# A list scheduler's ranks: program order before, latest begins from a backward walk after

## The chip, the cores and the metric

The kernel runs on one NeuronCore of a Trainium2 chip. The metric is the device time of one execution in microseconds; three runs of the kernel before give a median of 1071.82 us.

## The reference

Three stages follow each other; the first one's output is the second one's input, and so on.

```python
# attention: batch 4, heads 8, sequence 576, head size 64, float32
scores = q @ k.T / sqrt(64)
thresh = max(scores, axis=-1) - tau                 # tau = 0.02
scores = where(scores >= thresh, scores, -1e9)
attn   = exp(scores - max(scores)); attn /= sum(attn) + 1e-9
x      = (attn @ v)  -> (2304, 512)
# gated layer, weights 512 x 1536 (and 1536 x 512), float64 in memory
x = (sigmoid(x @ w_gate) * (x @ w_val)) @ w_out
# second layer, w1, w2: 512 x 1024, w3: 1024 x 1024, w_out2: 1024 x 512
out = ((x @ w1) * (x @ w2) @ w3) @ w_out2
```

## The kernel before

**Attention.** The 4 batches hold 4 pairs of heads each, so 16 pairs; a pair takes 9 steps (four blocks of 128 queries per head and one block of the tails), 144 steps in all, 36 a batch. A step g is: the scores on TensorE into one of two PSUM buffers (`s_mm`, L618), the row maximum less tau on DVE (`s_max`, L648), the threshold and the exponential on ACT (`s_exp`, L656 and L657), a split of the result into two f16 halves (`s_hi` on ACT at L668 or DVE at L666, `s_lo` mostly on POOL at L674), a transposing DMA (`s_tr`, L678), and five steps later the product with v (`pv`, L681). Each value of q, k and v is split in a high and a low part, which costs each pair some ACT, DVE and POOL work ahead of its steps (`q_act`, `q_dve`, `k_act`, `k_dve`, `v_max` to `v_split`). After 9 steps the pair is normalised (L699), transposed (L717) and written to `XA` (`x_act`, L732 and L734).

**Filler.** Between the parts of a step the program calls `filler` twice (L1217 and L1230), which emits other work for TensorE. First that is the product w3 @ w_out2 (`merge_gen`, L803), which takes 24 units of float64 weights, cast by DVE, ACT and POOL at L762 to L771 (`cast64`), and needs no attention. When all of it is emitted, its pool `mp` closes, and the pools of the gated layer open in its place (the planner's `over`). Then `l1_gen` (L903) emits the gated layer in passes: pass b works on batch b, and its first step, `xsplit` (L968), reads what `x_act` of batch b wrote. Pass 0 also casts the 36 units of the layer's float64 weights, at 2 POOL operations a unit (L771 and L781), and stores them as float32 for the passes after it. Pass 3 comes behind attention.

**The planner.** All instructions up to `cut` (L1231, the end of the attention loop with its fillers) are put in a new order by `Plan` (L22 to L304). `edges` finds the dependencies of the written program: `hard` ones (data and buffer reuse) and `soft` ones (order of allocation, and PSUM accesses of one engine). `time` has a cost for each operation. `order` (L207) walks forwards in time: of all engines it takes the one whose best instruction could start first; on an engine that is the instruction with the least wait until it is surely ready, and among those ready the one with the lowest `rank` (L229). The rank is the place in the written program, as `BY` is 0 (L50, L1125):

```python
self.rank = [n + by * (i.name in behind) for n, i in enumerate(self.x)]
...
n = min(avail[e], key=lambda n: (max(sure[n] - free[e] - 1, 0), self.rank[n]))
```

`pin` (L297) fixes the order found on each of the engines PE, DVE, ACT, POOL and on SP, which issues all DMAs. The order is worked out when the program is built; the chip runs each engine's list in that order, with semaphores for the dependencies.

Behind the cut come pass 3 of the gated layer, the splitting of w1 and w2, and the second layer. They are not planned by `Plan`.

Of the kernel before, what the change touches and what calls it, by code (L numbers as in the profile page):

```python
# [21 lines left out]
class Plan:  # L22
# [9 lines left out]
    CLK = 3413.0  # L32
    SLACK = {"DMACopy": 3000.0, "DmaTransposeAnt": 1500.0}
    HOLD = 200.0

    def __init__(self, insts, cut, over, late=(), by=0):
        self.later = [i for i in insts[cut:] if i.opcode in self.OPS]
        insts = insts[:cut]
        self.x = [i for i in insts if i.opcode in self.OPS and self.name(i.engine) in self.ENG]
        self.e = [self.ENG[self.name(i.engine)] for i in self.x]  # L40
        self.io = [
            ([o.bass_ap for o in i.ins if hasattr(o, "bass_ap")],
             [o.bass_ap for o in i.outs if hasattr(o, "bass_ap")])
            for i in self.x
        ]
        self.hard = [set() for _ in self.x]
        self.soft = [set() for _ in self.x]
        self.edges(over)
        behind = {insts[i].name for a, b in late for i in range(a, min(b, cut))}
        self.rank = [n + by * (i.name in behind) for n, i in enumerate(self.x)]  # L50
        self.cost = [self.time(n) for n in range(len(self.x))]

    @staticmethod
    def name(e):
# [119 lines left out]
    def time(self, n):  # L174
        x, e = self.x[n], self.e[n]
        ins, o = self.io[n][0], self.io[n][1][0]
        k = max(self.free(o), self.free(ins[0]) if ins else 0)
        sb = [self.place(a) != "PSUM" for a in ins] or [True]
        if e == "SP":
            if x.opcode == "DmaTransposeAnt":  # L180
                return 1440, 1152 * 18.8 / 16, 702, 1305, 1152
            c, r = self.packets(o, ins[0])
            one = max(r / (22.0 if r <= 2048 else 18.0) + 5, 48 if r >= 512 else 0) + (40 if c == 64 else 0)
            return 530, c * one / 16, 1055, 1285, c
        if e == "PE":
            f = all(str(a.dtype).endswith("float32") for a in ins)
            h = self.size(ins[0]) == 2
            iv = 29 if k <= 64 else 108 if f else 39 if h else k / 2.4 + 13
            return iv, 165 + iv, k / 2.4 * (2 if f else 1)
        if e == "ACT":  # L190
            ptr = len(ins) > 1
            return 167 + (30 if sb[0] else 0) + (85 if ptr and k > 1 else 60 if ptr else 0) + k / 1.2 + 95 * (
                len(self.io[n][1]) - 1
            ), 0, 0
        if e == "POOL":
            if len(ins) < 2:
                return 110 + 0.95 * k, 0, 0
            return (150 + 2.0 * k if self.size(o) == 2 else 160 + 2.2 * k), 0, 0
        if self.free(o) == 128 and k > 576:
            return 1280, 0, 0  # L200
        port = all(sb) and self.place(o) != "PSUM" and k > 1 and (
            x.opcode in ("TensorTensor", "TensorCopy") or self.size(ins[-1]) == 2
        )
        more = len(self.io[n][1]) > 1 or any(self.free(a) == 1 for a in ins)
        return 148 + (k / 0.96 + (60 if more else 0) if k > 1 else 0), port, 0

    def order(self):  # L207
# [16 lines left out]
        while left:  # L224
# [55 lines left out]
            for m in succ[n]:  # L280
                need[m] -= 1
                if not need[m]:
                    r = t = max((start[q] for q in self.soft[m]), default=0.0)
                    for q in self.hard[m]:
# [3 lines left out]
                        else:  # L288
                            u = done[q] + self.LAG[self.e[q]] + self.LEAD[self.e[m]]
                            r = max(r, u)  # L290
                            t = max(t, u + self.SLACK.get(self.x[q].opcode, self.HOLD))
                    ready[m], sure[m] = r, t
                    avail[self.e[m]].append(m)
        self.start, self.done = start, done
        return seq

    def pin(self, tc):  # L297
        for e, l in self.order().items():
            for m, n in zip(l, l[1:]):
                tc.add_manual_dep(  # L300
                    self.x[n], self.x[m].name,
                    mybir.DependencyInfo(mybir.DependencyClass.NoSync, mybir.DependencyReason.DATA),
                    reason="order",
                )  # L304
# [1198 lines left out]
```

## Time and profile before

| | us |
|---|---|
| median of three runs (lowest, highest) | 1071.82 (1071.23, 1078.38) |
| the profiled execution's own time | 1074.56 |
| its span, first to last instruction | 1072.8 |
| TensorE busy in the span | 1004.5 |
| VectorE (DVE), ScalarE (ACT), GpSimd (POOL) busy | 673.1, 663.7, 692.4 |

Busy times are sums over the span; what an engine is worth is read in each stretch by itself. [...]

### The profile page before, as it was taken

The numbers are of one execution on the slowest core, as the hardware profiler recorded it, in microseconds if no ns is written. First come the engines' busy times: TensorE is split into PE (matmuls) and PEld (weight loads), VectorE is DVE, ScalarE is ACT, GpSimd is POOL, SyncE is SP. The second block draws the span as 40 slices with busy tenths as digits, with TensorE's granted clock in tenths as the row PEclk, the third lists the DMA queues.
The fourth block names the chain that finished last, engine by engine and source line by source line (L and its number), as shares of the span: only waits on it lengthen the run. The fifth ranks groups of instructions, "written<-read, shape, count | busy, mean of one in ns | idle before, by whom it ended". The sixth has DMA issues, their size and how long they took to land. (4 is left out here: it accounts for less than half of the span.)

```text
span 1072.8 us, 20181 instructions
## 1 busy us (share of the span) xinstructions
PE 1004.5 (94%) x7088; PEld 891.5 (83%) x7088; DVE 673.1 (63%) x1226; ACT 663.7 (62%) x1325; POOL 692.4 (65%) x587
## 2 busy tenths in 40 slices
PE   4599976899998999999999989999999999999997
PEld 3488865687887888888888879999999989989995
DVE  8896587777866655557554447776776725743741
ACT  6687699978879878879887664445432322422221
POOL 5966288899997777667766756767664723552530
PEclk9999969999999999999999999999999999999999
DMA  8899699999999999989987675767378619835822
GB/s 218 237 238 226 146 234 220 254 224 268 252 251 228 219 211 223 209 191 210 232 171 164 130 178 186 255 223 236 129 248 276 204 60 321 258 98 173 310 78 59
DMA packets 301844, 221.28 MB, mean 206 GB/s; under 512 B 221872, under 2 KB 250544, under 8 KB 301744
## 3 DMA queue, kind: packets, MB, share of 16 engines
q1 hardware_dynamic: 301744, 220.00, 80.9%
q8 instruction: 56, 0.92, 0.4%
q14 instruction: 44, 0.36, 0.1%
HBM read 133.17 MB, written 30.93 MB: 153 GB/s over the span
## 5 line engine op out<-in xcount | busy, mean ns | idle before, releaser
L674 POOL TENSOR_TENSOR h<-e,h 128x576 f16<-128x576 f32 x120 | 155.1, 1295 | 75.7 <-ACT h L668 43.0
L648 DVE TENSOR_SCALAR_CACHE_REDUCE e<-ps_s,tauc 128x576 f32<-128x576 f32 x144 | 117.1, 814 | 72.2 <-PE ps_s L348 31.9
L656 ACT ACTIVATE ps_s<-ps_s,nt 128x576 f32<-128x576 f32 x144 | 102.4, 712 | 50.0 <-DVE e L648 48.4
L657 ACT ACTIVATE e<-ps_s,ebias 128x576 f32<-128x576 f32 x144 | 106.5, 740 | 2.9 <-POOL vl L781 0.4
L348 PEld LDWEIGHTS <-pt 128*128 128x128 f16 x2240 | 76.7, 100 | 32.6 <-issue 23.1
L348 PE MATMUL ps_h<-xl,gh 128*128 128x512 f32 (+1 forms) x240 | 93.1, 388 | 3.9 <-POOL xl L781 2.8
L348 PE MATMUL ps_h<-xl,vh 128*128 128x512 f32 (+1 forms) x240 | 92.5, 385 | 0.0
L348 PE MATMUL ps_y<-wm,abh 128*128 128x512 f32 x288 | 91.4, 390 | 0.3 <-DVE wm L781 0.3
L348 PE MATMUL ps_o<-gvl,oh 128*128 128x512 f32 (+1 forms) x240 | 90.7, 378 | 0.0
L348 PE MATMUL ps_h<-xh,gh 128*128 128x512 f32 (+1 forms) x240 | 89.1, 371 | 0.0
L348 PE MATMUL ps_h<-xh,gl 128*128 128x512 f32 (+1 forms) x240 | 88.9, 371 | 0.0
L348 PE MATMUL ps_h<-xh,vh 128*128 128x512 f32 (+1 forms) x240 | 88.8, 370 | 0.0
L348 PE MATMUL ps_h<-xh,vl 128*128 128x512 f32 (+1 forms) x240 | 88.8, 370 | 0.0
L348 PE MATMUL ps_o<-gvh,ol 128*128 128x512 f32 (+1 forms) x240 | 88.5, 369 | 0.0
L348 PE MATMUL ps_o<-gvh,oh 128*128 128x512 f32 (+1 forms) x240 | 88.3, 369 | 0.0
L668 ACT ACTIVATE h<-e 128x576 f16<-128x576 f32 x126 | 86.0, 684 | 2.9 <-DMA pt<-h 1.5
L781 POOL TENSOR_TENSOR gl<-w,gh 128x512 fp32r<-128x512 f32 x42 | 55.0, 1310 | 49.3 <-ACT gh L780 48.7
L781 POOL TENSOR_TENSOR gvl<-gr,gvh 128x512 fp32r<-128x512 f32 (+1 forms) x48 | 60.3, 1256 | 10.2 <-ACT gvh L780 9.6
L780 ACT ACTIVATE abh<-r 128x384 fp32r<-128x384 f32 x48 | 24.2, 521 | 68.9 <-DVE r L1368 68.6
L781 POOL TENSOR_TENSOR ol<-w,oh 128x512 fp32r<-128x512 f32 x42 | 55.8, 1336 | 16.7 <-ACT oh L780 16.7
L781 POOL TENSOR_TENSOR vl<-w,vh 128x512 fp32r<-128x512 f32 x43 | 58.1, 1352 | 8.7 <-ACT vh L780 8.4
L348 PEld LDWEIGHTS ps_y<-wm,abh 128*128 128x128 f32 x288 | 54.0, 188 | 11.4 <-DVE wm L781 0.6
(208 smaller groups left out, 3021.0 us busy)
## 6 DMA issues: line engine op xcount, KB each, us to landing
wc<-sc_c SPq DMA_DIRECT2D x168, 256.0 KB, 3.4
w<-sc_w SPq DMA_DIRECT2D x35, 768.0 KB, 5.2
sc_c<-wc SPq DMA_DIRECT2D x56, 256.0 KB, 2.7
XR<-in_moe_w_out_dram SPq DMA_DIRECT2D x20, 512.0 KB, 4.9
sc_w<-w SPq DMA_DIRECT2D x11, 768.0 KB, 5.9
XR<-in_moe_w_dram SPq DMA_DIRECT2D x16, 512.0 KB, 4.7
raw<-in_moe_w_dram SPq DMA_DIRECT2D x16, 512.0 KB, 4.6
XR<-in_moe_w_gate_dram SPq DMA_DIRECT2D x12, 512.0 KB, 5.5
```

Of the source, the lines that this page charges most:

```text
L348: nc.tensor.matmul(out_, lhsT, rhs, start=first, stop=last)
L648: nc.vector.tensor_scalar(e, x["ps"], tauc, None, op0=ALU.add, op1=ALU.min, accum_out=nt)
L656: nc.scalar.activation(x["ps"], x["ps"], AF.Prelu, scale=-1.0, bias=x["nt"], alpha=STEEP)
L657: nc.scalar.activation(x["e"], x["ps"], AF.Exp, bias=ebias, accum_out=prep[pr]["sum"][:, s:s + 1])
L668: nc.scalar.activation(x["h16"][:, 0:S], x["e"], AF.Copy)
L674: eng.tensor_tensor(hb[:, S:2 * S], st[g]["e"], hb[:, 0:S], op=ALU.subtract)
L780: nc.scalar.activation(hi, x, AF.Copy)
L781: (lo_eng or nc.gpsimd).tensor_tensor(lo, x, hi.bitcast(F32), op=ALU.subtract)
```

## The change

`Plan` gets a method `backward`, and `pin` runs `order` and `backward` in turn twice before the last `order`. `backward` schedules the same instructions in reversed time, from those with no successor, with the durations that the forward walk gave (`lat`) and the time for which each holds its engine (`held`). Of an engine's candidates it takes the one with the least wait, among equals the one that the forward walk finished last. The instructions are then sorted by how far before the end they must begin, and that place is their new `rank`. The rule by which `order` picks is unchanged, as are the instructions, the tiles, the buffers and everything behind the cut. Two more pieces come along: an argument `beads`, for which no caller passes anything, and a cost for matmuls with operands of 64 partitions.

```diff
+    ROUNDS = 2
-    def __init__(self, insts, cut, over, late=(), by=0):
+    def __init__(self, insts, cut, over, late=(), by=0, beads=()):
...
+        for row in beads:
+            row = [at[insts[i].name] for i in row]
+            for m, n in zip(row, row[1:]):
+                self.soft[n].add(m)
+                self.hard[n].discard(m)
...
+            if ins[0].ap[0][1] == 64 and k > 128:
+                side = ins[0].offset * self.size(ins[0]) // (ins[0].tensor.bytes() // 128) >= 64
+                return (4 if side else k / 2.4 + 11), 290, k / 2.4 * (0 if side else 1)
...
+    def backward(self):
+        N, E = len(self.x), ("PE", "DVE", "ACT", "POOL", "SP")
+        pred = [self.hard[n] | self.soft[n] for n in range(N)]
+        out = [0] * N
+        for n in range(N):
+            for q in pred[n]:
+                out[q] += 1
+        lat = [d - s for s, d in zip(self.start, self.done)]
+        held = [
+            c[0] if e in ("PE", "SP") else max(60, c[0] - self.OVER[e])
+            for c, e in zip(self.cost, self.e)
+        ]
+        ready, begin = [0.0] * N, [0.0] * N
+        avail = {e: [n for n in range(N) if not out[n] and self.e[n] == e] for e in E}
+        free = dict.fromkeys(E, 0.0)
+        for _ in range(N):
+            best = None
+            for e in E:
+                if not avail[e]:
+                    continue
+                n = min(avail[e], key=lambda n: (
+                    max(ready[n] + lat[n] - held[n] - free[e] - 1, 0), -self.done[n]
+                ))
+                s = max(free[e], ready[n] + lat[n] - held[n])
+                if best is None or s < best[0]:
+                    best = s, e, n
+            s, e, n = best
+            avail[e].remove(n)
+            begin[n] = free[e] = s + held[n]
+            for q in pred[n]:
+                out[q] -= 1
+                if q not in self.hard[n]:
+                    r = begin[n] - lat[q]
+                elif self.e[q] == self.e[n] != "SP":
+                    r = begin[n] - (lat[q] - 5 if e == "PE" else 0)
+                else:
+                    r = begin[n] + self.LAG[self.e[q]] + self.LEAD[e]
+                ready[q] = max(ready[q], r)
+                if not out[q]:
+                    avail[self.e[q]].append(q)
+        for i, n in enumerate(sorted(range(N), key=lambda n: -begin[n])):
+            self.rank[n] = i
+
     def pin(self, tc):
+        for _ in range(self.ROUNDS):
+            self.order()
+            self.backward()
         for e, l in self.order().items():
```

## Rows read from the trace of the kernel before

**Rows 1.** Page, its first part: busy us, share, instructions of each engine.

```profile
PE 1004.5 (94%) x7088; PEld 891.5 (83%) x7088; DVE 673.1 (63%) x1226; ACT 663.7 (62%) x1325; POOL 692.4 (65%) x587
```

**Rows 2.** Chain that ended last, in order of time: start us, us, what.

```profile
631.84 0.31 ACT XR L734
...
632.23 0.53 ACT xh L780
...
632.83 1.01 POOL xl L781
...
633.88 8.59 PE ps_h L348 x48
```

**Rows 3.** Windows view of the whole core, by stage.

```profile
core 0: us, PE busy (x) PEld busy (x) DVE busy (x) ACT busy (x) POOL busy (x), PEclk, DMA share, GB/s
0.00:50.00 50.00, 22.40 (x109) 19.06 (x110) 41.83 (x82) 32.66 (x62) 37.09 (x44) 1.00 0.82 224
50.00:100.00 50.00, 49.05 (x394) 41.91 (x393) 41.42 (x78) 40.97 (x80) 34.04 (x29) 1.00 1.10 231
100.00:125.00 25.00, 22.29 (x182) 19.04 (x181) 12.79 (x27) 16.89 (x35) 7.88 (x7) 0.93 0.80 189
125.00:178.00 53.00, 38.61 (x414) 34.45 (x413) 39.49 (x84) 46.86 (x96) 40.00 (x34) 0.81 0.96 210
178.00:225.00 47.00, 40.39 (x366) 33.71 (x363) 34.81 (x76) 43.45 (x92) 40.56 (x34) 0.96 1.09 239
225.00:325.00 100.00, 98.81 (x776) 82.47 (x775) 72.75 (x140) 79.68 (x158) 93.71 (x77) 1.00 1.06 254
325.00:350.00 25.00, 21.27 (x226) 17.70 (x224) 15.86 (x36) 23.60 (x50) 19.29 (x16) 0.93 1.07 222
350.00:475.00 125.00, 125.00 (x981) 103.12 (x977) 71.85 (x145) 101.17 (x201) 87.44 (x71) 1.00 1.02 212
...
500.00:625.00 125.00, 125.00 (x986) 102.63 (x985) 65.05 (x130) 97.80 (x194) 85.75 (x70) 1.00 0.85 179
...
632.50:1072.80 440.30, 431.50 (x2340) 412.26 (x2340) 258.99 (x394) 152.52 (x309) 224.65 (x195) 1.00 0.60 195
```

**Rows 4.** Windows view of line L648 alone (DVE); two instructions are one step.

```profile
50.00:75.00 25.00, 4.90 (x12) 1.00 1.07 238
...
125.00:150.00 25.00, 4.94 (x12) 0.82 0.80 185
150.00:175.00 25.00, 6.59 (x16) 0.78 1.12 234
```

**Rows 5.** Windows view of tile ps, the merge's PSUM banks.

```profile
50.00:75.00 25.00, 20.06 (x95) 14.96 (x93) 4.12 (x6) 4.63 (x8) 1.00 1.07 238
...
125.00:150.00 25.00, 4.57 (x18) 3.25 (x18) 0.00 (x0) 0.60 (x1) 0.82 0.80 185
```

**Rows 6.** Timeline of PE, 170 to 192 us: the first matmul of pass 0.

```profile
181.00 0.49 PE L348 MATMUL ps_h<-xl,gh 128*128 128x512 f32 x1
```

**Rows 7.** Waits of PE, 100 to 225 us: us in total, times, longest.

```profile
PE ps_s L348 <- ACT e L657: 8.0, 6, 1.8
PE ps_s L348 <- DVE qbd L515: 4.0, 2, 2.8
...
PE ps L348 <- DVE tl L847: 2.7, 1, 2.7
```

**Rows 8.** Waits, two of the longest by DMA or cast: DVE 100 to 125, PE 0 to 50.

```profile
DVE vm L568 <- DMA vnat<-in_v_dram: 4.0, 1, 4.0
...
PE ps L842 <- POOL f L771: 7.5, 1, 7.5
```

**Rows 9.** Lines L771 and L666: ns min/median/max, first and last start us.

```profile
L771 POOL TENSOR_TENSOR w<-w,t x36: 1249/1288/1498, 139.0 to 332.0; 128x512 int32<-128x512 int32 x36
...
L666 DVE CAST h<-e x18: 452/939/2944, 21.4 to 312.4; 128x576 f16<-128x576 f32 x18
```

**Rows 10.** Groups of POOL, 225 to 325 us.

```profile
L674 POOL TENSOR_TENSOR h<-e,h 128x576 f16<-128x576 f32 x21 | 27.5, 1316 | 3.7 <-ACT h L668 2.7 <-ACT t L767 0.5 <-DVE h L666 0.4
...
L781 POOL TENSOR_TENSOR vl<-w,vh 128x512 fp32r<-128x512 f32 x8 | 10.4, 1295 | 0.9 <-ACT vh L780 0.9
```

More of the change, by code (lines that the diff above doesn't have):

```diff
@@ L48, in __init__ @@
         self.edges(over)
+        at = {i.name: n for n, i in enumerate(self.x)}
+        for row in beads:
[3 more added lines that the diff above has]
+                self.hard[n].discard(m)
+        ends = set()
+        for row in beads:
+            ends |= {at[insts[row[1]].name], at[insts[row[-1]].name]}
         behind = {insts[i].name for a, b in late for i in range(a, min(b, cut))}
@@ L51, in __init__ @@
         self.cost = [self.time(n) for n in range(len(self.x))]
+        for n in ends:
+            self.cost[n] = self.cost[n][0] + 100, *self.cost[n][1:]
     @staticmethod
```

## The prediction

> **What bounds the kernel now.** I read the page's engine shares first: TensorE is busy for 94% of the span, no other engine for more than 65% [rows 1]. Whatever order the planner finds, TensorE's work stays, so what can be won is its idle time and the time that it runs at the lower clock. The chain comes next [rows 2]: it begins at 631.84 us with the last write of attention, goes through the split of that batch, and from 633.88 is TensorE alone. So the kernel's time is the end of attention plus a tail. The tail lies behind the cut; TensorE is busy for 431.5 of its 440.3 us [rows 3], and the planner does not touch it. I carry it over unchanged.
>
> The windows by stage [rows 3] then say where TensorE is idle in the planned part: 27.6 us in the first 50, 0.95 in 50 to 100, 2.7 in 100 to 125, 14.4 in 125 to 178, 6.6 in 178 to 225, 1.2 in 225 to 325, 3.7 in 325 to 350, and nothing in 350 to 475 or 500 to 625. Nearly all that an order can still mend lies before 350 us.
>
> Why is it idle there? The merge product is the only filler until batch 0 of attention is done. It takes 20.06 of 25 us early and its last 4.57 us fall in 125 to 150 [rows 5], while the next filler, pass 0, starts its first matmul at 181.00 [rows 6]. Between them TensorE has attention alone, and waits for ACT's exponential and for DVE [rows 7]; ACT is busy for 46.86 of 53 us [rows 3]. Attention makes 6 steps in 25 us while the merge runs, 8 when it has gone [rows 4]. So TensorE is full first and starved later. Pass 0, once it runs, loads another engine: POOL is busy for 93.71 of 100 us in 225 to 325 [rows 3].
>
> **The change, part by part.** No instruction is added or removed, so every term is a wait that goes, comes or moves. `beads` is never passed and costs nothing. The cost for operands of 64 partitions matches no matmul: those of pass 0, the merge and attention load all 128 rows (the 128*128 in [rows 6]). What is left is the ranks. The walk still never leaves an engine idle when something is surely ready, so a rank decides only between instructions that are ready together. I expect it to matter where four engines are all half full and queues are long, before 178 us, and little where TensorE is full anyway.
>
> *The stretch 50 to 178.* By program order, casts and merge matmuls emitted at step g go ahead of attention's step g+3. A latest begin puts ahead what has the longest way to the end: attention's chain of scores, maximum, exponential, split and transpose, and the casts of pass 0, and puts back what has slack. Every instruction that is moved takes its own DMAs along on SP. TensorE's idle time here is 0.95 + 2.7 + 14.4 = 18.05 us. As a check from the other side: the 24 steps of 50 to 150 at 6 in 25 us take 100 us; at 7 (half way to the 8 of [rows 4]) they would take 24/7 x 25 = 85.7, some 14 us less, of which the idle 18.05 has room. At the least nothing is won; at the most all 18; and if attention made 5.5 steps instead of 6, 24/5.5 x 25 - 100 = 9 us would be lost. I take half of the idle time, 9.0.
>
> *The stretch 178 to 350.* Idle are 6.6 + 1.2 + 3.7 = 11.5 us. Part of it is the end of pass 0 before batch 1 is done (325 to 350), which better balance would mend. POOL limits it: casts and splits of 36 units at about 1.29 us an operation run from 139 to 332 us [rows 9, 10], and no rank makes them shorter. I take a third, 4.0; bounds 0 and 11.5 for the gain; the loss is the second rival's.
>
> *The clock.* The granted clock is 0.93, 0.81, 0.96 and 0.93 in four of these stretches [rows 3]. [...] But there it waits for ACT and DVE, so faster matmuls only make the waits longer: I take 0 of 0 to 15.4, and keep it for the low end.
>
> *The first 50 us.* 27.6 us idle, the longest wait being 7.5 for a merge cast [rows 8]. Loads and the chain of the first pair set this; I take 0, between 7.5 won and 5 lost (one more wait like that for `qbd`, of which the longest was 2.8 [rows 7], on either of two pairs).
>
> *New stalls.* An order is as good as the planner's durations. Now DVE stands 4.0 us before `vm` for a load, with others queued behind it, and TensorE 2.7 us for `tl` [rows 7, 8]: both are waits in a fixed order that hardly any planner would choose. The new order loses these and gets others. I take them as equal: 0, within 6.7 either way.
>
> The sum: 9.0 + 4.0 = 13 us. The profiled execution took 1074.56 us, so 1061.6 for one like it; the median of the runs shown lies 2.7 below that execution, which makes 1058.8, say 1059.
>
> [...] The casts of L666 on DVE take 452 ns at best, 939 in the median and 2944 at worst [rows 9], with POOL at work beside the slow ones. [...]
>
> **Rivals.** *First: nothing that can be measured (within 1%, 10.7 us, is about what a measurement of this kernel can't tell from no change).* For it: ACT is 88% busy in 125 to 178, so batch 0 may be bound by ACT and not by order, and the walk already fills every gap that it sees. Against it: ACT has 9 us free in 50 to 100 and 8 in 100 to 125 [rows 3]. Then only a third of the terms comes, 4 us: 1068, from 1062 to 1078.
>
> *Second: slower, by POOL in pass 0.* Where: 225 to 325 us, POOL 93.71 of 100 busy, TensorE 98.81. Each unit of weights needs two POOL operations and each step of attention one more at L674 [rows 10]. If the ranks put attention's L674 ahead of a unit's split, TensorE stands at the next matmul for half an operation, 0.65 us, on average: 36 x 0.65 = 23 us, some of it at the lower clock. Less 9 us from the first term, 14 lost net: 1086. It decides from the point at which more than about 14 of the 36 units arrive late (14 x 0.65 = 9). For it: the 6% of slack. Against it: both walks know POOL's costs, and POOL is busy for only 41.9 of the 75 us from 50 to 125, so an order that starts pass 0's casts sooner eases it.
>
> *Third: the ranks come out as program order nearly does.* The program was emitted with attention and filler interleaved, and the reverse walk breaks ties by the forward one. Then 1071, within 4. Against it: 24 casts of the merge are emitted within few steps, long before they are due.
>
> **How the numbers follow.** The forecast 0.48, the first rival 0.24, the second 0.19, the third 0.09. The forecast's own range is 1042 to 1061. Toward the low end it would need the whole 29.6 us of idle time in 50 to 350 and some of the clock: 1072 - 30 - 4 = 1038. Toward the high end I take in the first and third rival and the mildest form of the second: 1081. So 1038 to 1081. Faster by over 1% is the forecast, 0.48; within 1% the first and third rival, 0.33; slower by over 1% is the second, 0.19.
>
> **What would show it.** Right: the first `ps_h` matmul well before 181 us, near 172; more steps than 6 in 25 us at L648 between 50 and 125; idle of TensorE in 125 to 178 about half; the last L734 near 619 instead of 631.84; the tail still 440 us. Wrong: waits of `ps_h` on POOL's or DVE's splits in 225 to 325; a new wait for a DMA in 350 to 625, where there was none; or a tail of another length, which I have as given.

## The result, and the profile after

| | before | after |
|---|---|---|
| median of the runs, us | 1072.13 (1069.01 to 1078.38, 6 runs) | 1063.70 (1062.98 to 1065.36, 6 runs) |
| ratio to before, 95% interval | | 0.9917 [0.9895, 0.9939] |
| profiled execution; its span, us | 1074.56; 1072.8 | 1065.11; 1063.3 |

The change makes the kernel faster by 0.8%: 8.4 us between the medians, 9.5 between the spans. That is the forecast direction, 4.7 us above the forecast time of 1059 and inside the whole range, but above the forecast's own range of 1042 to 1061.

The changed kernel has other line numbers: L348, L648, L666, L674, L678, L752 and L771 of before are L409, L709, L727, L735, L739, L813 and L832 here. This is its windows view by the stages of [rows 3] (its columns are those of [rows 3]; PEclk is the granted TensorE clock as a share of full speed); the row to 622.80 ends where pass 3 begins.

```profile
0.00:50.00 50.00, 24.92 (x118) 20.25 (x119) 43.70 (x88) 35.05 (x66) 40.42 (x46) 0.76 0.88 234
50.00:125.00 75.00, 75.00 (x634) 64.97 (x633) 54.70 (x109) 60.83 (x120) 41.26 (x34) 1.00 0.97 222
125.00:178.00 53.00, 39.51 (x412) 34.38 (x411) 43.25 (x90) 50.39 (x104) 43.49 (x37) 0.81 1.04 226
178.00:225.00 47.00, 42.77 (x377) 35.41 (x376) 37.66 (x68) 38.27 (x79) 40.90 (x34) 0.93 0.96 230
225.00:350.00 125.00, 122.02 (x979) 100.88 (x978) 93.12 (x180) 106.18 (x214) 111.62 (x90) 0.99 1.01 240
350.00:500.00 150.00, 149.91 (x1241) 123.86 (x1240) 91.85 (x183) 128.16 (x260) 110.40 (x88) 1.00 1.02 218
500.00:622.80 122.80, 119.90 (x999) 98.18 (x998) 58.98 (x120) 93.30 (x183) 83.66 (x68) 1.00 0.83 182
622.80:1063.30 440.50, 433.05 (x2340) 413.80 (x2340) 258.12 (x394) 151.49 (x306) 223.90 (x194) 0.99 0.59 193
```

The first number after the stretch's length is TensorE's busy time. Idle time is length less busy. Against [rows 3]: 25.1 us instead of 27.6 in the first 50; none instead of 3.7 in 50 to 125; 13.5 instead of 14.4 in 125 to 178; 4.2 instead of 6.6 in 178 to 225; 3.0 instead of 4.9 in 225 to 350. From 350 us on 0.7 less. Up to the start of pass 3 TensorE is idle for 48.8 us instead of 60.9, so 12.1 are won; it is busy for 1.0 us more; and the tail is 440.5 us instead of 438.9. 12.1 - 1.0 - 1.6 is the 9.5 us between the spans.

The tail's 1.6 us lie at its first matmuls. The chain that ended last shows them for the changed kernel (start us, us, what), to be held against the 8.59 us of [rows 2]; the granted clock in 625 to 650 was 0.97, where before had 1.00.

```profile
207.76 5.41 issue
...
622.82 10.16 PE ps_h L409 x48
```

The other piece of that chain, at 207.76, is a stall that before did not have; the experiments come back to it. The first matmul of pass 0, which stood at 181.00 us [rows 6], in the changed kernel's timeline:

```profile
169.28 0.77 PE L409 MATMUL ps_h<-xl,gh 128*128 128x512 f32 x1
```

A useful set of milestones is the last write of each batch by attention, L732 before and L793 after (every fourth of its 16 starts in the timeline):

| end of batch | 0 | 1 | 2 | 3 |
|---|---|---|---|---|
| before, us | 182.47 | 339.00 | 492.50 | 630.95 |
| after, us | 170.74 | 334.09 | 479.54 | 620.39 |
| lead of after | 11.7 | 4.9 | 13.0 | 10.6 |

So attention wins 11.7 us in batch 0, loses 6.8 of them in batch 1 and wins 8.1 in batch 2. This is attention's place in the order and not time won or lost as such: in batch 2, from 350 to 500, TensorE is full in both kernels (0.8 us idle before, 0.1 after).

**Where batch 0's gain comes from.** A difference shows at once on SP's timeline. These are its first transposes and the weight loads around them, before (start us, us, operation, count):

```profile
18.84 1.57 SPq L678 DMA_TRANSPOSE pt<-h  x1
...
29.33 12.69 SPq L752 DMA_DIRECT2D XR<-in_moe_w_dram  x6
42.11 1.32 SPq L678 DMA_TRANSPOSE pt<-h  x1
```

and after:

```profile
19.05 1.40 SPq L739 DMA_TRANSPOSE pt<-h  x1
...
30.55 1.35 SPq L739 DMA_TRANSPOSE pt<-h  x1
32.09 11.41 SPq L813 DMA_DIRECT2D XR<-in_moe_w_dram  x5
```

Before, the second transpose stands on SP behind six loads of merge weights, issued from 29.33 to 42.02. But the loads are not what it waited for. It needs POOL's split of the same step, and that stands on POOL's timeline before:

```profile
39.17 1.27 POOL L771 TENSOR_TENSOR f<-t,t 128x512 int32<-128x512 int32 x1
40.39 1.29 POOL L674 TENSOR_TENSOR h<-e,h 128x576 f16<-128x576 f32 x1
```

and after:

```profile
28.21 1.28 POOL L735 TENSOR_TENSOR h<-e,h 128x576 f16<-128x576 f32 x1 [0.40 <-DVE h L727]
```

Before, DVE's cast of that step had ended at 24.32 (21.38 + 2.94). POOL ran eleven operations of the merge first, from 24.40 on, and the split ended at 41.68, 0.43 us ahead of the transpose. After, the split starts 0.08 us behind its cast. That is attention passing the merge on POOL, as forecast.

Most of this early lead is lost again, though. These are the starts of the row maximum (L648 before, L709 after) of some steps, counted from 0:

| step | 6 | 12 | 16 | 20 | 28 | 36 |
|---|---|---|---|---|---|---|
| before, us | 50.95 | 75.84 | 89.88 | 113.73 | 144.08 | 170.64 |
| after, us | 44.53 | 73.11 | 86.93 | 105.87 | 132.02 | 158.74 |
| lead of after | 6.4 | 2.7 | 3.0 | 7.9 | 12.1 | 11.9 |

Of the lead that lasts, 4.9 us come between steps 16 and 20. There DVE waited before for the load of the next pair's v [rows 8], with the row maxima queued behind, and after it does not (DVE's timelines, before and then after):

```profile
106.93 1.23 DVE L568 TENSOR_REDUCE vm<-vnat 128x128 bf16<-128x640 f32 x1 [3.99 <-DMA vnat<-in_v_dram]
```

```profile
103.04 1.30 DVE L629 TENSOR_REDUCE vm<-vnat 128x128 bf16<-128x640 f32 x1
```

On SP the last of the three loads of that v is issued at 103.59 before and at 97.89 after. That this wait makes up the 4.9 us is read from the traces; no run tried it alone. The 4.2 us from step 20 to step 28 were not traced further.

### The profile page after: what moved, and what is told of

It is laid out like the page before. It is cut to its first block, busy times and chain, and to the rows that moved or that the text cites. A ratio compares the mean times of both kernels' runs of the same rounds, so it can differ in the third digit from the quotient of the medians.

```text
span 1063.3 us, 20140 instructions
## 1 busy us (share of the span) xinstructions
PE 1007.1 (95%) x7088; PEld 891.7 (84%) x7088; DVE 681.4 (64%) x1226; ACT 663.7 (62%) x1325; POOL 695.6 (65%) x587
## 4 chain that ended last, share of the span: by engine, by line
PE 86%; ACT 4%; DVE 4%; issue 2%; POOL 2%; DMA 1%; SPq 1%; DVEq 0%; ACTq 0%; POOLq 0%
PE ps_h L409 28%; PE ps_ab L409 15%; PE ps_o L409 14%; PE ps_s L409 9%; PE ps_y L409 8%; PE u L409 4%; PE ps L409 4%; PE ps_t L524 1%; ACT e L718 1%; ACT ps_s L717 1%; PE ps_x L782 1%; DVE e L709 1%; PE ps L903 1%; DMA XR<-in_moe_w_out_dram 1%; DMA XR<-in_moe_w_val_dram 0%
## 5 line engine op out<-in xcount | busy, mean ns | idle before, releaser
L735 POOL TENSOR_TENSOR h<-e,h 128x576 f16<-128x576 f32 x120 | 156.0, 1303 | 61.9 <-ACT h L729 24.5
L709 DVE TENSOR_SCALAR_CACHE_REDUCE e<-ps_s,tauc 128x576 f32<-128x576 f32 x144 | 117.3, 815 | 72.7 <-PE ps_s L409 38.2
L409 PEld LDWEIGHTS <-pt 128*128 128x128 f16 x2240 | 77.4, 100 | 33.2 <-issue 24.7
L409 PE MATMUL ps_h<-xl,gh 128*128 128x512 f32 (+1 forms) x240 | 93.3, 389 | 2.5 <-POOL xl L842 2.5
L409 PE MATMUL ps_h<-xl,vh 128*128 128x512 f32 (+1 forms) x240 | 92.4, 385 | 0.0
L409 PE MATMUL ps_y<-wm,abh 128*128 128x512 f32 x288 | 91.4, 390 | 0.3 <-DVE wm L842 0.3
L409 PE MATMUL ps_o<-gvl,oh 128*128 128x512 f32 (+1 forms) x240 | 91.0, 380 | 0.0
L409 PE MATMUL ps_h<-xh,gl 128*128 128x512 f32 (+1 forms) x240 | 90.1, 375 | 0.6 <-POOL gl L842 0.6
L409 PE MATMUL ps_h<-xh,gh 128*128 128x512 f32 (+1 forms) x240 | 90.1, 375 | 0.0
L409 PE MATMUL ps_h<-xh,vl 128*128 128x512 f32 (+1 forms) x240 | 90.0, 375 | 0.0
L409 PE MATMUL ps_h<-xh,vh 128*128 128x512 f32 (+1 forms) x240 | 89.5, 373 | 0.0
L409 PE MATMUL ps_o<-gvh,ol 128*128 128x512 f32 (+1 forms) x240 | 88.9, 370 | 0.0
L409 PE MATMUL ps_o<-gvh,oh 128*128 128x512 f32 (+1 forms) x240 | 88.6, 370 | 0.0
L842 POOL TENSOR_TENSOR vl<-w,vh 128x512 fp32r<-128x512 f32 x43 | 58.0, 1349 | 11.3 <-ACT vh L841 11.2
L409 PEld LDWEIGHTS ps_y<-wm,abh 128*128 128x128 f32 x288 | 54.0, 188 | 11.4 <-DVE wm L842 0.6
```

Of the source, the lines that this page charges most:

```text
L409: nc.tensor.matmul(out_, lhsT, rhs, start=first, stop=last)
L709: nc.vector.tensor_scalar(e, x["ps"], tauc, None, op0=ALU.add, op1=ALU.min, accum_out=nt)
L735: eng.tensor_tensor(hb[:, S:2 * S], st[g]["e"], hb[:, 0:S], op=ALU.subtract)
L842: (lo_eng or nc.gpsimd).tensor_tensor(lo, x, hi.bitcast(F32), op=ALU.subtract)
```

## The experiments

All ratios are to the kernel before on the same chip, with their 95% intervals.

**e1 and e2: the ranks for one part of the program.** `front` marks the instructions emitted in the first 44 steps, which is batch 0 with the merge.

```diff
+        front = {i.name for i in insts[:late[2 * 44][0]]}
+        self.front = [i.name in front for i in self.x]
...
         for _ in range(self.ROUNDS):
             self.order()
             self.backward()
+        self.rank = [r if f else N + n for n, (r, f) in enumerate(zip(self.rank, self.front))]   # e1
+        self.rank = [N + r if not f else n for n, (r, f) in enumerate(zip(self.rank, self.front))]   # e2
```

> The new ranks for the instructions emitted in the first 44 steps alone (batch 0 and the merge); those emitted later keep program order behind them. Theory (the gain is made before pass 0 begins, by bringing its first ps_h matmul from 181 to 169 us): 1063 to 1066, with the first ps_h at 168 to 172. Rival (the gain is made later, by a better balance of pass 0 to 2 with attention): 1069 to 1074, whatever the first ps_h does.

Measured: 1066.02 us, ratio 0.9958 [0.9943, 0.9972]; first `ps_h` at 172.24.

> The converse: program order for the first 44 steps, the new ranks from there on. Theory: 1069 to 1073, first ps_h near 181. Rival (the gain is made later): 1062 to 1066 with the first ps_h still near 181.

Measured: 1078.40 us, ratio 1.0069 [1.0043, 1.0095]; first `ps_h` at 184.84. The first part alone brings half of the gain (0.42 of 0.83%), and the second alone loses, more than the theory allowed. So half of the gain is made early; the theory's claim that all of it is, is not borne out, and the second part is not neutral. Of the 4.7 us that e2's span is longer than that of before, 3.9 are idle time of TensorE in 225 to 325, where it is busy for 94.91 us (98.81 before) and DVE for 82.38 (72.75 before) with about the same number of instructions. The windows view of e2:

```profile
225.00:325.00 100.00, 94.91 (x733) 78.85 (x734) 82.38 (x144) 76.82 (x152) 85.66 (x70) 0.98 0.93 231
```

**e3 and e4: the ranks on SP alone, and on all but SP.** A rank is compared only within one engine's list, so the two can be mixed. They do not separate cleanly, though: the walk plans all engines together, so new ranks on SP move the others' instructions too. In e3's trace ACT's order departs from that of before at its second operation and POOL's at its 20th.

```diff
             self.order()
             self.backward()
+        self.rank = [r if e == "SP" else n for n, (r, e) in enumerate(zip(self.rank, self.e))]   # e3
+        self.rank = [r if e != "SP" else n for n, (r, e) in enumerate(zip(self.rank, self.e))]   # e4
```

> The new ranks on SP's queue of DMAs alone, program order on the four engines. Theory (what wins is attention ahead of merge casts on ACT, DVE and POOL): within 3 us of before, 1069 to 1075. Rival (what wins is that transposes go ahead of weight loads in the one DMA queue): 1063 to 1067.

Measured: 1067.51 us, ratio 0.9970 [0.9953, 0.9987]; first `ps_h` at 173.71.

> The converse: the new ranks on PE, ACT, DVE and POOL, program order on SP. Theory: 1062 to 1067, as after. Rival (the DMA queue's order is what wins): 1069 to 1075.

Measured: 1072.80 us (1066.68 to 1077.41), ratio 1.0019 [0.9999, 1.0039]; first `ps_h` at 178.13. Here my theory fell: e3 lies outside its range and half a us above the rival's, and e4 is the rival's case. Ranks on SP alone move the first `ps_h` by 7.3 of the 11.7 us, ranks on the four engines alone by 2.9, and only the former is faster in time. Neither alone gives the 0.83% of both. How much of e3's gain is the DMA queue itself stays open, since the engines' orders moved along; and e4's trace, of an execution of 1068.17 us, holds a stall of the kind described next, so it does not show that the engines' order is worth nothing.

**What is long on DVE.** Looking for DVE operations over 2 us, I found that the changed kernel, e2 and e4 each have one cast of 5.7 to 6.7 us near 205 to 220 us, and before, e1 and e3 have none there. In the changed kernel's timeline this is the cast, and TensorE's wait of its waits view in 178 to 225:

```profile
206.59 6.66 DVE L727 CAST h<-e 128x576 f16<-128x576 f32 x1
```

```profile
PE ps_s L409 <- DVE vx L642: 4.2, 1, 4.2
```

and POOL in the same stretch (idle time before an operation stands in brackets at its end):

```profile
206.73 1.29 POOL L832 TENSOR_TENSOR w<-w,t 128x512 int32<-128x512 int32 x1
207.96 1.30 POOL L735 TENSOR_TENSOR h<-e,h 128x576 f16<-128x576 f32 x1
209.22 1.28 POOL L832 TENSOR_TENSOR w<-w,t 128x512 int32<-128x512 int32 x1
210.45 1.26 POOL L842 TENSOR_TENSOR gvl<-gr,gvh 128x512 fp32r<-128x512 f32 x1
211.67 1.26 POOL L842 TENSOR_TENSOR gl<-w,gh 128x512 fp32r<-128x512 f32 x1
215.36 1.28 POOL L842 TENSOR_TENSOR vl<-w,vh 128x512 fp32r<-128x512 f32 x1 [2.43 <-ACT vh L841]
```

The cast ends at 213.25, just after POOL's unbroken run ends at 212.93; at its best it takes 0.45 us. Five POOL operations, one after another, begin and end while it lasts. The planner counts at most the rest of one POOL operation as a cast's wait. Behind the stall TensorE also runs slower: its granted clock reads 0.50 from 214 to 220 us, and matmuls of 288 columns that followed each other at 0.13 us near 206 us do so at 0.24 near 215. The next runs try this.

**e5 to e7: no casts on DVE.**

```diff
-        if b < 2 and g % 4 == 1:
+        if b < 0:        # e5 in the changed kernel, e6 in the kernel before
+        if b < 1 and g % 4 == 1:        # e7, changed kernel
             nc.vector.tensor_copy(x["h16"][:, 0:S], x["e"])
```

> The changed kernel with all of s_hi on ACT: the 18 casts on DVE of batches 0 and 1 become 18 ACT operations of 0.68 us. Theory (a cast on DVE can't begin while POOL's operations follow each other without a gap; the one of 6.66 us at 206.59 holds TensorE for 4.2 us): no wait for DVE over 2.5 us in 178 to 225, and 1058 to 1062. Rival (ACT, busy for 50.39 of 53 us in 125 to 178, is what bounds batch 0, and gets 12 us more work): 1066 to 1073.

Measured: 1077.13 us, ratio 1.0061 [1.0032, 1.0089].

> The same edit in the kernel before, whose longest cast on DVE took 2.94 us. Theory (before had no long block to lose): 1071 to 1080, no better than before and worse by up to the ACT work of batch 0. Rival (the casts cost both kernels alike): 1064 to 1068.

Measured: 1078.16 us (1068.51 to 1080.50), ratio 1.0039 [1.0008, 1.0069].

> The changed kernel with the casts on DVE in batch 0 alone (9 of 18); those of batch 1, the blocked one among them, go to ACT. Theory: 1058 to 1062, with no wait of TensorE over 2.5 us in 178 to 225, and at least as fast as with all casts on ACT, as ACT gets no more work in batch 0. Rival (the 4.2 us are made good later anyway, since POOL limits pass 0): 1062 to 1066.

Measured: 1078.78 us, ratio 1.0064 [1.0044, 1.0084]. All three came out slow, e5 and e7 by 13 and 15 us over the changed kernel and above both of the ranges expected for them. By its direction e5 is the rival's case, but e7 is not: it has no more ACT work in batch 0, its first `ps_h` stands at 169.62 and its batch 1 is what is late. The view by line of `rs` (ns min/median/max), the addition of 1e-9 times 1024 to the row sums in `x_norm`, shows a second operation that is long at times. In e7:

```profile
L763 DVE TENSOR_SCALAR rs<-sum x16: 157/176/9554, 57.1 to 619.6; 128x9 f32<-128x9 f32 x16
```

and around its longest, on e7's timelines of DVE and POOL:

```profile
226.19 9.55 DVE L763 TENSOR_SCALAR rs<-sum 128x9 f32<-128x9 f32 x1
235.78 0.22 DVE L764 RECIPROCAL rs<-rs 128x9 f32<-128x9 f32 x1
```

```profile
225.54 1.30 POOL L735 TENSOR_TENSOR h<-e,h 128x576 f16<-128x576 f32 x1
226.78 1.56 POOL L670 TENSOR_TENSOR vl<-vnat,vh 128x512 f16<-128x512 f32 x2
228.28 1.30 POOL L735 TENSOR_TENSOR h<-e,h 128x576 f16<-128x576 f32 x1
229.53 1.30 POOL L832 TENSOR_TENSOR w<-w,t 128x512 int32<-128x512 int32 x1
230.78 1.27 POOL L842 TENSOR_TENSOR gl<-w,gh 128x512 fp32r<-128x512 f32 x1
232.00 1.28 POOL L735 TENSOR_TENSOR h<-e,h 128x576 f16<-128x576 f32 x1
233.23 1.27 POOL L842 TENSOR_TENSOR vl<-w,vh 128x512 fp32r<-128x512 f32 x1
234.45 1.27 POOL L832 TENSOR_TENSOR w<-w,t 128x512 int32<-128x512 int32 x1
```

An operation on 9 columns, 0.16 us at best, stands for 9.55 us and ends as POOL's run does, at 235.7. In e5 it takes up to 9.40 us, in e6 6.60, in e2 7.33; before at most 1.21, after 1.22. The planner counts no wait for POOL at this operation.

Up to 640 us, 35 of these casts and additions took more than 1.8 us in the 14 kernels together; those of 4 us and more are called blocks here. Each of the 22 casts ends 0.32 us, and each of the 13 additions 0.03 us, after the end of a POOL operation. In 33 of them POOL's unbroken run ends there; in two (e2 at 283.33, e12 at 223.08) it goes on. So "can't begin" in e5's theory is more than the traces show: they show when these operations end, and not what makes them last.

**e9 and e11: the same without that addition.**

```diff
-        nc.vector.tensor_scalar(rs, p["sum"], 1e-9 * PSC, None, op0=ALU.add)
-        nc.vector.reciprocal(rs, rs)
+        nc.vector.reciprocal(rs, p["sum"])        # e9: with e5's edit; e11: with e7's
```

> As e5 (all of s_hi on ACT), and x_norm takes the reciprocal of the sums directly: the addition of 1e-9 times 1024, an operation of 128x9 on DVE alone that took up to 9.40 us in e5, is left out. Theory (what made e5 slow is that this operation, like the casts, stands until POOL has a gap, and all of DVE's queue behind it): no operation of DVE over 2.5 us in 125 to 350, and 1056 to 1066, over 10 us less than e5. Rival (e5 was slow because ACT bounds batches 0 and 1): 1072 to 1078, as e5.

Measured: 1065.93 us, ratio 0.9955 [0.9937, 0.9973]; no DVE operation over 2 us up to 640 us. That is 11 us under e5 by the medians, so most of e5's loss came with the addition's blocks, not with ACT's work. What ACT's extra work costs shows earlier: the first `ps_h` stands at 174.22, against 169.18 in e11 below, which has the nine casts of batch 0 on DVE.

> As e7 (casts on DVE in batch 0 alone), and without the addition in x_norm, which took up to 9.55 us in e7. Theory (blocks of DVE by POOL's unbroken run made e7 slow and cost the changed kernel some 4 us): no operation of DVE over 3.5 us in 50 to 350, and 1057 to 1063, that is 15 us under e7 and under the changed kernel's 1063.7. Rival (the block in the changed kernel was made good later, so nothing is left to win): 1063 to 1068.

Measured: 1059.12 us, ratio 0.9865 [0.9816, 0.9913]; the longest DVE operation in 50 to 350 is 2.80 us. It is 20 us under e7 and 4.6 under the changed kernel; the intervals of these last two overlap (0.9913 against 0.9895). Its windows view in pass 0 shows TensorE hardly ever idle, where after had lost 3.0 us in 225 to 350:

```profile
225.00:325.00 100.00, 99.86 (x821) 84.02 (x820) 70.38 (x141) 87.74 (x175) 96.05 (x80) 1.00 1.06 249
325.00:350.00 25.00, 25.00 (x210) 20.87 (x209) 16.49 (x38) 23.09 (x48) 16.29 (x13) 1.00 1.13 234
```

Its batches end 10.5, 13.9, 19.0 and 16.9 us ahead of before: the loss in batch 1 is gone. It is not simply the 4.2 us given back: in 178 to 225 TensorE is idle for 4.5 us here too, of which 3.7 are a wait for ACT.

**e8, e10 and e12: another draw of the order.** `HOLD` is a planning allowance of 200 ns; 5 ns less means nothing on the chip, but gives another order.

```diff
-    HOLD = 200.0
+    HOLD = 195.0        # e8 changed kernel; e10 kernel before; e12 e8 with e9's edit of x_norm
```

> The changed kernel with the planner's HOLD at 195 instead of 200, which says nothing about the chip but draws another order. Theory (the ranks by latest begins are better as such): 1060 to 1068. Rival (8 us are the luck of one draw of an order): anywhere from 1060 to 1078, 1069 or more as likely as not.

Measured: 1059.47 us, ratio 0.9887 [0.9859, 0.9916].

> The kernel before with HOLD at 195 instead of 200: another order of the same kind, ranked by program order. Theory (the ranks make the difference, not the draw): 1068 to 1076, above both draws with the new ranks (1063.7 and 1059.5). Rival (draws differ by as much as the change): 1060 to 1066, or over 1078.

Measured: 1075.23 us, ratio 1.0041 [1.0021, 1.0062].

> As e8 (the changed kernel with HOLD at 195, 1059.5), and without the addition in x_norm, which was not blocked in e8. Theory (where it is not blocked it costs next to nothing, and what moves the time then is the draw of the order): 1056 to 1065. Rival (the addition costs each of 16 pairs something anyway): 1050 to 1056.

Measured: 1058.53 us, ratio 0.9867 [0.9810, 0.9924]. Two draws with program order lie at 1.000 and 1.0041, two with latest begins at 0.9917 and 0.9887: the draws of one rule differ by 0.3 to 0.4%, the rules by 0.8 to 1.5%. Two of each are few, but the rival that the gain is luck is not borne out. It is not ruled out either: e10's order is close to that of before (POOL's first 160 operations are the same), and e5 and e7, whose ranks are latest begins too, lie at 1.006. e12 is as fast as e11; both medians are below the changed kernel's, but the intervals of e8, e11 and e12 all overlap with its own. e8 holds a cast of 4.75 us at 298.77 and is no slower than e12, which has none over 2.3, so a block does not always cost time. The kernel before without the addition was not run.

## Why the prediction was right, and where it was off

*What bounds the kernel* held: all that changed lies before pass 3, 11.3 of the 12.1 us of idle time before 350 us, and no instruction was added. The last write of the kind that begins [rows 2] came at 619.8, where 619 was forecast.

*The direction and the first `ps_h`.* Forecast near 172, measured 169.28. Attention did run ahead of the merge.

*The stretch 50 to 178 was mis-sized:* 9.0 us taken, 4.6 came (3.7 in 50 to 125, 0.9 in 125 to 178). TensorE was filled completely where I had expected little, and the starved stretch behind it stayed. Between the last merge matmul and the first `ps_h` ACT is busy for 44.5 of 45.9 us (47.4 of 50.7 before), and by e9 against e11, whose orders differ too, nine more casts on ACT, 6.1 us of work, put the first `ps_h` 5.0 us later. So the first rival was right for that stretch in the changed kernel: ACT, and no longer order, bounds the end of batch 0. In the kernel before it was order: the same casts on ACT (e6) leave the first `ps_h` no later there, at 172.07 instead of 181.00, in the one execution traced (1070.42 us). Two signs that I had named failed with it. The idle time of 125 to 178 was not halved. And attention made 5, 6 and 6.5 steps in the three pieces of 25 us from 50 to 125 instead of more than 6; it ran faster only behind them, with 8 and 9 instead of 6 and 8.

*The reason for the gain was incomplete.* I had attention pass the merge on the engines, and noted only that DMAs move along. On POOL it did pass the merge, but most of that lead is gone by step 12. Of the lead that lasts, 4.9 us come where the load of v is issued earlier, a wait that I had listed under new stalls and set equal to those that come. The first 50 us, where I took 0, gave 2.5.

*The stretch 178 to 350:* 4.0 taken, 4.3 came.

*The clock:* taken as 0 of 0 to 15.4. No run shows that 15.4 us can come back. What the traces show, in windows of 1 us from 50 to 350: the clock reads 0.50 in 26 of the 300 and 1.00 in 264 before, 0.50 in 26 and 1.00 in 265 after, and values between in the rest; the time at 0.50 adds up to 30.7 us in both, of which 15.4 is half. Behind 350 it cost 1.6 us at the start of the tail. Why TensorE is busy for 1.0 us more up to pass 3 is not shown.

*New stalls were taken as equal to those that go,* 0 within 6.7. The cast of 6.66 us holds TensorE for 4.2, which is all of its idle time in 178 to 225. No term of the sum is for long casts, of which [rows 9] shows one of 2.94 us. In batch 0 no cast took over 3.24 us; the long one came in batch 1, once, and longer than any row had shown. Whether it makes up the 4.6 us by which the change fell short is not shown: e11, without such blocks, is 4.6 us faster, but e8, another draw with a block of its own, is 4.2 us faster too.

*The number* is near for several reasons that partly cancel. Idle time won, by stretch: 2.5 (0 taken) + 4.6 (9.0) + 4.3 (4.0) + 0.7 (0) = 12.1 us; less 1.0 of busy time and 1.6 of tail, that is the 9.5 between the spans where the sum had 13. That the time came within 5 us of 1059 is in part luck.

*The chances.* The forecast's mechanism came at two thirds of its size, 0.83%. By the prediction's own division that is not the forecast (faster by over 1%) but the class of the first and third rival (within 1%), and 1063.7 is as near to the first rival's 1068 as to 1059. It was told from no change all the same: the interval ends at 0.9939. The second rival, POOL holding up pass 0, came in another form: not splits that are late (TensorE waits for POOL's splits for 0.6 us in 225 to 350), but casts and additions on DVE that last until a POOL operation ends, in 33 of 35 the last of an unbroken run. By e5 and e7, against e9 and e11, that form can turn the change into a loss of 0.6%. e2 loses 0.7% with three such blocks (5.75, 7.33 and 4.50 us), but was not tried without them.

What stays open: which of the engines' lists brings how much, what the stall in batch 1 costs by itself, and why batch 2 wins 8.1 us with the new ranks.

## What to carry to other kernels

A list schedule's ranks act on every queue that it orders, the DMA queue too: look for loads that an engine stands waiting for and see how late they were issued. When a transfer stands behind others in the queue, check when its data was ready before blaming the queue. Beside a POOL without gaps, DVE's casts of 128x576 took up to 6.66 us here (0.45 at best) and its additions of 128x9 up to 9.55 (0.16 at best): when POOL is packed more densely, look in the trace for such operations from SBUF to SBUF, however small, and try a kernel without them (e9 is 11 us faster than e5, e11 20 us faster than e7), or with them on ACT, if ACT has room. And when orders are compared, draw a second one of each kind, since here two draws differ by 3 to 4 us, and by 15 where one has several blocks.

## What the runs showed of the hardware that was not expected

A DVE operation of 128x9 elements from SBUF to SBUF took 9.55 us (e7), and a cast of 128x576 took 6.66 (the changed kernel), each ending within 0.4 us of the end of an unbroken run of POOL operations. Not every operation from SBUF to SBUF was long beside POOL: in the changed kernel 13 of the 16 TENSOR_REDUCE of 128x640 (L629) begin while a POOL operation runs and none takes over 1.34 us (1.27 at best), and 7 of the 16 RECIPROCAL of 128x9 (L764) lie within one and take 0.22 at most (0.20 at best).

The granted clock in the windows view of before does not fit its matmuls in the first 50 us: it reads 1.00 there [rows 3], yet at 31 to 33 us matmuls of 288 columns follow each other at 0.24 us. They do so at 0.24 us too at 143 to 145 us, where the clock of before reads 0.50, and in the changed kernel at 0.13 us near 206 us, where it reads 1.00. So those at 31 to 33 us ran at about half the full clock. The rows of after read 0.76 in the same stretch. The two were therefore not compared there.
